# Chunk attention with a feed-forward layer: when w_in is issued, how far ahead loads go, and which blocks the crossbar transposes

## The chip, the cores and the metric

The kernel runs on one core of a Trainium2 chip. The metric is the time of one execution on the device in microseconds (us). A core has TensorE (matmuls; PE in the profile, PEld its weight loads), VectorE (DVE), ScalarE (ACT), GpSimd (POOL) and SyncE (SP, which here only issues DMAs). They run side by side, each with its own instruction list in order, and wait for each other through semaphores.

## The reference

```python
B, H, S, D = 8, 8, 576, 64; chunk = 64
scores = (1 / sqrt(D)) * q_c @ k_c.T          # within chunks of 64 tokens, per head
scores = scores - scores.max(-1, keepdims=True)
attn = exp(scores); attn = attn / (attn.sum(-1, keepdims=True) + 1e-9)
out = attn @ v_c                              # (B, H, S, D)
x = out.transpose(0, 2, 1, 3).reshape(B * S, H * D)   # 4608 x 512
h = x @ w_in                                  # w_in 512 x 2048
g = maximum(0.01 * h, h)
return g @ w_out                              # w_out 2048 x 512
```

All inputs and the output are float32.

## The kernel before

The 4608 tokens are cut into nine blocks of 512 (`NJ = 9`, `TB = 512`); a block is eight chunks of 64 over all eight heads. Heads are handled in pairs, `kk` = 0 to 3 (`NKK = 4`). A block j passes through these stages:

- `alloc(j)` takes the float32 landing tiles `qf`, `kf`, `vf` (two sets) and the float16 tiles `qh`, `kh` (two sets). `load_qk` and `load_v` (L106, L120) issue the loads, mostly from SyncE. A block seldom begins at the start of a sequence of 576, so most loads split in two: v then takes 16 issues for a block, q and k four.
- `cast_qk` and `cast_v` turn them into float16, v into `VD[j % 2]`. `VD` holds the two heads of a pair as a block diagonal, whose other half is cleared once by memsets (L65 to 67).
- `attn_t` (L174) brings q and k into the layout with the head dimension on the partitions. For j < `NPT` TensorE does this (eight transposes into the PSUM tile `tp`, from which VectorE copies `qt` and the two halves of `kd`; for block 0 ScalarE copies one half). For later blocks `transpose(j)` (L163) has issued two DMA transposes, called the crossbar here.
- `attn_s` forms the scores in `sp` and their exponential `e`; `attn_x` the sums `zp` and the product with v, `xp`, and then 1/sum on ScalarE (`lz`, `rz`); `attn_n` multiplies `xp` by `rz` on VectorE into `xT`.
- `mm1(j, fc)` is one of 16 column groups of the first product (four matmuls over `kk`), ended by ScalarE's leaky ReLU into `gT`. `mm2(j, ti, part)` is a quarter of one of four row tiles of the second product (four matmuls). After a tile's last quarter VectorE copies it into `osb` (three buffers) and SyncE stores it.

The program is written in one order by hand, and every engine runs its instructions in that order. In a block's loop n runs over 32 steps, 16 `mm1` and 16 `mm2`. Between them stand the four attention stages of the next block for each pair (`at`, from `first`, `gap` and `lags`), the loads of a later block (`loads`), the casts of block j + 2 (from step `cast_at`), and its crossbar transposes (12 steps later). Block 0's second product runs its quarters part by part over all four tiles, and so all four of its output tiles end close together; the later blocks go tile by tile.

Before the loop, block 0's attention runs pair by pair: at each step the casts of one pair, its transposes, the scores of the pair before and so on, with `keep_warm` matmuls on zeros in between and with the first three columns of the first product at the end. w_in and w_out come as float32 and land as float16 by DMAs from GpSimd, four groups each (`load_w_in(g)`, `load_w_out(g)`, 1 MB read and 512 KB written each). w_in's groups 0 to 2 are issued behind GpSimd's casts of pairs 1 to 3, and its group 3 and all of w_out after the last pair. Block 1's loads then wait for w_in's group 2 (`add_manual_dep`, L336): v first, then q and k in two halves.

Of the kernel before, what the change touches and what calls it, by code (L numbers as in the profile page):

```python
# [9 lines left out]
FP32 = mybir.dt.float32  # L10
# [5 lines left out]
def kernel(  # L16
# [9 lines left out]
    nc = tc.nc  # L26

    B, H, S, D = q.shape
# [4 lines left out]
    NKK = H // 2  # L33
# [3 lines left out]
    NC = TB // CH  # L37
    R = 4
    NI = CH // R
    NPT = 4  # L40
    SCL = float(D) ** -0.5

    sb = ctx.enter_context(tc.tile_pool(name="sb", bufs=1))
# [21 lines left out]
    for t, eng in zip(VD, (nc.vector, nc.gpsimd)):  # L65
        eng.memset(t[0:64, :, :, 1, :], 0.0)
        eng.memset(t[64:128, :, :, 0, :], 0.0)
# [88 lines left out]
    def cast_v(j, kk):  # L156
        for hh in range(2):
            rows = slice(hh * CH, (hh + 1) * CH)
            nc.gpsimd.tensor_copy(  # L159
                out=VD[j % NVD][rows, kk, :, hh, :], in_=raw[j][2][rows, kk, :, :]  # L160
            )

    def transpose(j):  # L163

# [9 lines left out]
    def attn_t(j, kk):  # L174

        if j < NPT:
            tp = psum([128, 2, R, 128], FP16, "tp", "at")
            for a in range(2):
                for r in range(R):
                    nc.tensor.transpose(  # L180
                        out=tp[:, a, r, :], in_=half[j][a][:, kk, r, :, :], identity=ident
                    )
            qt = sbuf([128, R, 128], FP16, "qt", 2)
            nc.vector.tensor_copy(out=qt, in_=tp[:, 0, :, :])  # L184
            kt = tp[:, 1, :, :]
        else:
            qt, kt = (t[:, kk, :, :] for t in trans[j])
        kd = KD[(j * NKK + kk) % NKD]
        for hh in range(2):
            p0 = hh * 64  # L190
            dst = kd[p0:p0 + 64, :, hh, :].rearrange("p c (i r) -> p c i r", r=R)
            src = kt[p0:p0 + 64, :, :].rearrange("p r (c i) -> p c i r", i=NI)
            if j == 0 and hh == 0:
                nc.scalar.activation(out=dst, in_=src, func=AFT.Copy, bias=0.0, scale=1.0)  # L194
            else:
                nc.vector.tensor_copy(out=dst, in_=src)  # L196
        live[j, kk] = (qt, kd)
# [70 lines left out]
    def mm2(j, ti, part):  # L268
        if part == 0:
            op[j, ti] = psum([128, d_model], FP32, "op", "mm")  # L270
        o = op[j, ti]
        for fc in range(part * 4, part * 4 + 4):
            nc.tensor.matmul(  # L273
                out=o,
                lhsT=gT[j][:, fc, ti * 128:(ti + 1) * 128],
                rhs=w_out[:, fc, :],
                start=(fc == 0),
                stop=(fc == NFC - 1),
            )
        if part == 3:  # L280
            osb = sbuf([128, d_model], FP32, "osb", 3)
            nc.vector.tensor_copy(out=osb, in_=o)  # L282
# [9 lines left out]
    with tc.manual_schedule():  # L292

        alloc(0)
        for kk in range(NKK):
            load_qk(0, 2 * kk, 2 * kk + 2)
        for h in range(4, H):
            load_v(0, h, nc.scalar)
        for h in range(4):
            load_v(0, h, nc.gpsimd)  # L300
        warm = psum([128, TB], FP32, "warm", "mm")
        keep_warm(10)
        w_dma = []
        hps = [psum([128, TB], FP32, "hp", "mm") for _ in range(3)]
        for step in range(NKK + 3):
            p = step - 2
            if 0 <= p < NKK:
                attn_x(0, p)
            p = step - 1
            if 0 <= p < NKK:  # L310
                attn_s(0, p)
            p = step
            if p < NKK:
                cast_qk(0, 0, p, nc.vector)
                cast_qk(1, 0, p, nc.gpsimd)
# [26 lines left out]
        for h in range(1, H):  # L342
            load_v(1, h, nc.sync)
        load_qk(1, 0, H // 2)
        load_qk(1, H // 2, H)
        for kk in range(NKK):
            cast_v(1, kk)
        for kk in range(NKK):
            cast_qk(0, 1, kk, nc.gpsimd)
            cast_qk(1, 1, kk, nc.gpsimd)  # L350

        for j in range(NJ):

            loads = {0: ((2, 16),), 1: ((3, 0), (4, 16))}.get(j, ((j + 3, 0),))

            first, gap, lags = (
                (24, 2, (0, 3, 5, 7)),
                (9, 5, (0, 3, 5, 7)),  # L360
                (6, 6, (0, 3, 5, 7)),
                (0, 7, (0, 3, 5, 7)),
            )[min(j, 3)]
            at: dict[int, list] = {}
            if j + 1 < NJ:
                for s in (3, 2, 1, 0):
                    for kk in range(NKK):
                        at.setdefault(first + gap * kk + lags[s], []).append((STEPS[s], kk))
            cast_at = (32, 24, 8, 2)[min(j, 3)]
            for n in range(NFC * 2 + (6 if j == 0 else 0)):  # L370
                if n >= 2 * NFC:
                    pass
                elif n >= NFC:
# [4 lines left out]
                for jl, n0 in loads:  # L378
                    if jl < NJ and n == n0:
                        alloc(jl)  # L380
                        load_qk(jl, 0, H)
                    if jl < NJ and n - n0 in range(1, 2 * H, 2):
# [3 lines left out]
                if j and j + 2 < NJ and n in range(cast_at, cast_at + 8, 2):  # L386
# [12 lines left out]

# [28 lines left out]
```

## Time and profile before

| | |
|---|---|
| median of three runs | 325.39 us (325.23 to 325.73) |
| profiled execution | 325.32 us, span 323.5 us, granted clock 0.968 |
| TensorE busy | 296.1 us, 92% of the span |
| VectorE, ScalarE, GpSimd busy | 111.6, 149.9, 83.8 us |
| HBM read, written | 36.70 MB, 9.44 MB |
| chain of waits by engine | PE 75%, DMA 16%, SyncE's queue 4% |

The page of the profile describes one execution. It has the busy time of each engine, the span in 40 slices of 8.09 us, and the chain of work that ended last, followed back from the last instruction. The timeline lists instructions in order of time: start, length, engine, line, operation, what is written from what, and in brackets how long the engine had been idle and for whom. A window row gives, for a stretch of time, the busy time of each engine (with the count of instructions), then the granted clock of TensorE (1.00 is full), the mean busy share of the 16 DMA engines and the GB/s they moved. Matmul ends are modelled, so lengths of single matmuls overlap; starts are what to read.

### The profile page before, as it was taken

How to read it: one execution, taken by the hardware profiler on the slowest of the kernel's cores; microseconds unless marked ns; L12 is line 12 of the kernel's file. 1: busy time of each engine (PE TensorE's matmuls, PEld its weight loads, DVE VectorE, ACT ScalarE, POOL GpSimd, SP SyncE). 2: the span in 40 equal slices, each digit the busy share in tenths (PEclk: the TensorE clock that was granted, in tenths of full speed). 3: DMA queues.
4: the chain of work that ended last, by engine and by line, in shares of the span. 5: the costliest groups of instructions: out<-in, count | busy, mean ns of one | idle time of the engine just before them, and what ended most of it. 6: DMA issues, size and time to landing. Idle time of an engine off the chain costs nothing.

```text
span 323.5 us, 4923 instructions
## 1 busy us (share of the span) xinstructions
PE 296.1 (92%) x1911; PEld 145.2 (45%) x1911; DVE 111.6 (35%) x190; ACT 149.9 (46%) x257; POOL 83.8 (26%) x136
## 2 busy tenths in 40 slices
PE   6768968729999999999999999999999999999994
PEld 2434424414555455544444454454445444444441
DVE  5450004630354155442534453424523422420011
ACT  1476400425733474258427822872385248425500
POOL 9750335461642500620810251052100000000000
PEclk9799996958999999999999999999999999999999
DMA  7999979969789599799577975995118110010011
GB/s 219 217 186 191 169 194 248 181 204 209 138 189 219 139 200 153 156 243 207 120 192 190 167 134 170 288 177 148 65 27 105 65 67 0 32 67 32 0 67 65
DMA packets 88247, 47.25 MB, mean 146 GB/s; under 512 B 61088, under 2 KB 83616, under 8 KB 88224
## 3 DMA queue, kind: packets, MB, share of 16 engines
q1 hardware_dynamic: 79776, 41.96, 58.1%
q0 software_dynamic: 6336, 4.46, 9.3%
q10 hardware_dynamic: 2112, 0.52, 0.8%
q8 instruction: 15, 0.25, 0.3%
q14 instruction: 8, 0.07, 0.1%
HBM read 36.70 MB, written 9.44 MB: 143 GB/s over the span
## 4 chain that ended last, share of the span: by engine, by line
PE 75%; DMA 16%; SPq 4%; DVE 1%; issue 1%; ACT 1%; POOL 1%; DVEq 0%; POOLq 0%; ACTq 0%
PE op L273 34%; PE hp L247 34%; DMA kf<-in_k_dram 8%; DMA vf<-in_v_dram 4%; SPq L132 2%; DMA w_in<-in_moe_w_in_dram 2%; PE zp L219 2%; PE xp L222 2%; PE sp L204 2%; DMA qf<-in_q_dram 1%; PE tp L180 1%; SPq L111 1%; DMA out_dram<-osb 1%; DVE xT L240 1%; DVE osb L282 0%
## 5 line engine op out<-in xcount | busy, mean ns | idle before, releaser
L247 PE MATMUL hp<-xT,w_in 128*128 128x512 f16 x576 | 132.9, 383 | 3.3 <-DVE xT L240 3.3
L273 PE MATMUL op<-w_out,gT 128*128 128x512 f16 x576 | 134.3, 383 | 0.0
L258 ACT ACTIVATE gT<-hp 128x512 f16<-128x512 f32 x144 | 84.9, 596 | 56.2 <-PE hp L247 56.0
L247 PEld LDWEIGHTS <-w_in 128*128 128x128 f16 x576 | 54.8, 99 | 66.1 <-issue 6.7
L273 PEld LDWEIGHTS <-gT 128*128 128x128 f16 x576 | 54.4, 99 | 59.8 <-issue 2.1
L282 DVE COPY osb<-op 128x512 f32<-128x512 f32 x36 | 24.8, 691 | 86.7 <-PE op L273 80.4
L212 ACT ACTIVATE e<-sp 128x512 f16<-128x512 f32 x36 | 21.4, 594 | 56.2 <-PE sp L204 56.0
L151 POOL CAST kh<-kf 128x512 f16<-128x512 f32 x36 | 22.5, 626 | 86.8 <-DMA kf<-in_k_dram 52.8
L240 DVE TENSOR_TENSOR xT<-xp,rz 128x512 f16<-128x512 f32 x36 | 24.7, 690 | 53.4 <-ACT rz L232 53.0
L230 ACT ACTIVATE lz<-zp 128x512 f32<-128x512 f32 x36 | 21.4, 594 | 26.7 <-PE zp L219 26.7
L184 DVE COPY qt<-tp 128x512 f16<-128x512 f16 x16 | 6.8, 423 | 62.3 <-PE tp L180 62.3
L159 POOL CAST vd_75<-vf 64x512 f16<-64x512 f32 x36 | 23.0, 638 | 19.9 <-PE xp L222 10.7
L159 POOL CAST vd_76<-vf 64x512 f16<-64x512 f32 x32 | 19.8, 618 | 25.3 <-DMA vf<-in_v_dram 19.3
L232 ACT ACTIVATE rz<-lz 128x512 f32<-128x512 f32 x36 | 22.7, 630 | 6.6 <-DVE xT L240 5.5
L219 PE MATMUL zp<-e,onesd 128*128 128x512 f16 x36 | 14.1, 392 | 7.0 <-ACT e L212 7.0
L196 DVE COPY kd_73<-kT 64x512 f16<-64x512 f16 x20 | 13.8, 690 | 0.3
L196 DVE COPY kd_74<-kT 64x512 f16<-64x512 f16 x20 | 12.5, 627 | 0.3
L180 PE MATMUL tp<-ident,kh 128*128 128x128 f16 x64 | 6.9, 237 | 3.8 <-POOL kh L151 3.8
L151 POOL CAST qh<-qf 128x512 f16<-128x512 f32 x12 | 7.3, 611 | 11.3 <-DMA qf<-in_q_dram 10.9
L196 DVE COPY kd_73<-tp 64x512 f16<-64x512 f16 x14 | 9.6, 685 | 1.5 <-ACT kd_73 L194 1.3
L196 DVE COPY kd_74<-tp 64x512 f16<-64x512 f16 x14 | 9.6, 685 | 1.5 <-ACT kd_74 L194 1.3
L222 PEld LDWEIGHTS <-vd_75 128*128 128x128 f16 x160 | 7.3, 98 | 6.2 <-issue 1.7
(40 smaller groups left out, 108.3 us busy)
## 6 DMA issues: line engine op xcount, KB each, us to landing
out_dram<-osb SPq DMA_DIRECT2D x36, 256.0 KB, 2.8
w_in<-in_moe_w_in_dram POOLq DMA_DIRECT2D x4, 512.0 KB, 8.2
w_out<-in_moe_w_out_dram POOLq DMA_DIRECT2D x4, 512.0 KB, 15.0
vf<-in_v_dram SPq DMA_DIRECT2D x16, 112.0 KB, 5.0
qf<-in_q_dram SPq DMA_DIRECT2D x6, 256.0 KB, 7.4
kf<-in_k_dram SPq DMA_DIRECT2D x6, 256.0 KB, 8.0
qf<-in_q_dram SPq DMA_DIRECT2D x2, 768.0 KB, 9.2
kf<-in_k_dram SPq DMA_DIRECT2D x2, 768.0 KB, 11.9
```

The lines of the kernel that those rows point to most:

```text
L151: eng.tensor_copy(out=half[j][a][:, kk, :, :, :], in_=raw[j][a][:, 2 * kk:2 * kk + 2, :].rearrange("p h (r d) -> p r h d", r=R),)
L159: nc.gpsimd.tensor_copy(out=VD[j % NVD][rows, kk, :, hh, :], in_=raw[j][2][rows, kk, :, :])
L196: nc.vector.tensor_copy(out=dst, in_=src)
L212: nc.scalar.activation(out=e, in_=sp, func=AFT.Exp, bias=0.0, scale=SCL)
L219: nc.tensor.matmul(out=zp, lhsT=onesd, rhs=e, start=True, stop=True)
L230: nc.scalar.activation(out=lz, in_=zp, func=AFT.Ln, bias=0.0, scale=1.0)
L232: nc.scalar.activation(out=rz, in_=lz, func=AFT.Exp, bias=0.0, scale=-1.0)
L240: nc.vector.tensor_tensor(out=xT[j][:, kk, :], in0=xp.rearrange("p r t -> p (r t)"), in1=rz, op=ALU.mult)
L247: nc.tensor.matmul(out=hp, lhsT=w_in[:, kk, fc * 128:(fc + 1) * 128], rhs=xT[j][:, kk, :], start=(kk == 0), stop=(kk == NKK - 1),)
L258: nc.scalar.activation(out=gT[j][:, fc, :], in_=hp, func=AFT.Prelu, bias=0.0, scale=1.0, alpha=0.01)
L273: nc.tensor.matmul(out=o, lhsT=gT[j][:, fc, ti * 128:(ti + 1) * 128], rhs=w_out[:, fc, :], start=(fc == 0), stop=(fc == NFC - 1),)
L282: nc.vector.tensor_copy(out=osb, in_=o)
```

## The change

In block 0, q's casts of pairs 1 to 3 move from VectorE to GpSimd, k is cast ahead of q, and v of pairs 2 and 3 is cast after the last q. w_in's group 0 is issued behind the casts of the second pair, and groups 1, 2 and 3 behind those of the third. v's heads 4 to 7 of block 0 move from ScalarE's queue to SyncE's, behind q and k; the memsets of the second `VD` move behind the issues of w_out, also on GpSimd. Block 1's q and k are loaded whole, ahead of its v, and wait for w_in's group 1 (`w_dma[1]`). ScalarE copies its half of `kd` for even pairs only. `keep_warm` runs 8 at first and then 4 at a time. `osb` has four buffers.

In the loop, block 0 loads block 2 (q and k from step 24, v from 32, behind the stores); block 1 loads block 3; block 2 loads blocks 4 and 5; and from block 3 on it is three ahead as before. The attention steps of the next block move, the last multiply to step 34 in block 0 (behind its last `mm2`), 30 in block 1, 29 in block 2, and 28 as before from block 3 on. `NPT` goes from 4 to 5, so block 4 is transposed on TensorE and only the last four blocks by crossbar, 14 steps after `cast_at`.

```diff
-    NPT = 4
+    NPT = 5
...
-            if j == 0 and hh == 0:
+            if j == 0 and hh == 0 and kk % 2 == 0:
                 nc.scalar.activation(out=dst, in_=src, func=AFT.Copy, bias=0.0, scale=1.0)
...
-            osb = sbuf([128, d_model], FP32, "osb", 3)
+            osb = sbuf([128, d_model], FP32, "osb", 4)
...
-        for h in range(4, H):
-            load_v(0, h, nc.scalar)
         for h in range(4):
             load_v(0, h, nc.gpsimd)
+        for h in range(4, H):
+            load_v(0, h, nc.sync)
...
-        keep_warm(10)
+        keep_warm(8)
...
-                cast_qk(0, 0, p, nc.vector)
                 cast_qk(1, 0, p, nc.gpsimd)
-                if p >= 2:
-                    cast_v(0, p)
-                if p >= 1:
-                    w_dma.append(load_w_in(p - 1))
+                cast_qk(0, 0, p, nc.vector if p == 0 else nc.gpsimd)
+                if p in (1, 2):
+                    w_dma += [load_w_in(g) for g in ((0,), (1, 2, 3))[p - 1]]
+                if p == 3:
+                    cast_v(0, 2)
+                    cast_v(0, 3)
                 attn_t(0, p)
...
-                keep_warm(3)
+                keep_warm(4)
...
-        w_dma.append(load_w_in(3))
-        w_dma += [load_w_out(g) for g in range(4)]
+        for g in range(4):
+            load_w_out(g)
+        clear_vd(1, nc.gpsimd)
         alloc(1)
-        first_v = load_v(1, 0, nc.sync)[0]
         tc.add_manual_dep(
-            first_v.ins,
-            w_dma[2].ins.name,
+            load_qk(1, 0, H)[0].ins,
+            w_dma[1].ins.name,
...
-        for h in range(1, H):
+        for h in range(H):
             load_v(1, h, nc.sync)
-        load_qk(1, 0, H // 2)
-        load_qk(1, H // 2, H)
-        for kk in range(NKK):
-            cast_v(1, kk)
         for kk in range(NKK):
             cast_qk(0, 1, kk, nc.gpsimd)
             cast_qk(1, 1, kk, nc.gpsimd)
+        for kk in range(NKK):
+            cast_v(1, kk)
+
+        def regular(first, gap):
+            return [[first + gap * kk + lag for kk in range(NKK)] for lag in (0, 3, 5, 7)]
...
-            loads = {0: ((2, 16),), 1: ((3, 0), (4, 16))}.get(j, ((j + 3, 0),))
-
-            first, gap, lags = (
-                (24, 2, (0, 3, 5, 7)),
-                (9, 5, (0, 3, 5, 7)),
-                (6, 6, (0, 3, 5, 7)),
-                (0, 7, (0, 3, 5, 7)),
-            )[min(j, 3)]
+            qk_at = {0: {24: 2}, 1: {0: 3}, 2: {0: 4, 16: 5}}.get(j, {0: j + 3})
+            v_at = {0: {32: 2}, 1: {1: 3}, 2: {1: 4, 17: 5}}.get(j, {1: j + 3})
+            cast_at = {0: 40, 1: 20, 2: 18}.get(j, 2)
+            steps = {
+                0: [[21, 23, 25, 27], [24, 26, 28, 30], [26, 28, 30, 32], [28, 30, 32, 34]],
+                1: regular(8, 5),
+                2: regular(1, 7),
+            }.get(j, regular(0, 7))
...
-            cast_at = (32, 24, 8, 2)[min(j, 3)]
-            for n in range(NFC * 2 + (6 if j == 0 else 0)):
+            for n in range(NFC * 2 + (16 if j == 0 else 0)):
...
-                if n == cast_at + 12 and NPT <= j + 2 < NJ:
+                if NPT <= j + 2 < NJ and n == cast_at + 14:
                     transpose(j + 2)
-            if j == 0:
-                for kk in range(NKK):
-                    cast_qk(0, 2, kk, nc.gpsimd)
-                    cast_qk(1, 2, kk, nc.gpsimd)
-                    cast_v(2, kk)
```

Three places in the order of the engines matter below. The first is GpSimd during block 0's attention, from the first casts to the weights, before:

```order
L132 DMA vd_75<-in_v_dram 64x8x64 x4
L151 CAST kh<-kf 128x512 x2
L140 DMA w_in<-in_moe_w_in_dram 128x4x512
L151 CAST kh<-kf 128x512
L159 CAST vd_75<-vf 64x8x64 x2
L140 DMA w_in<-in_moe_w_in_dram 128x4x512
L151 CAST kh<-kf 128x512
L159 CAST vd_75<-vf 64x8x64 x2
L140 DMA w_in<-in_moe_w_in_dram 128x4x512 x2
L146 DMA w_out<-in_moe_w_out_dram 128x4x512 x4
```

and now:

```order
L154 CAST kh<-kf 128x512 x2
L154 CAST qh<-qf 128x512
L143 DMA w_in<-in_moe_w_in_dram 128x4x512
L154 CAST kh<-kf 128x512
L154 CAST qh<-qf 128x512
L143 DMA w_in<-in_moe_w_in_dram 128x4x512 x3
L154 CAST kh<-kf 128x512
L154 CAST qh<-qf 128x512
L163 CAST vd_75<-vf 64x8x64 x4
L149 DMA w_out<-in_moe_w_out_dram 128x4x512 x4
L67 MEMSET vd_76 64x32x64
```

Three q casts came to GpSimd, w_in's last three groups stand two k casts earlier or more, and a memset of `VD[1]` (`vd_76`) follows w_out.

The second is SyncE from block 0's last q and k on, before (the `64x64` and `64x7x64` are block 1's v, one head in two parts):

```order
L111 DMA qf<-in_q_dram 128x2x256
L111 DMA kf<-in_k_dram 128x2x256
L132 DMA vf<-in_v_dram 64x64
L132 DMA vf<-in_v_dram 64x7x64
L132 DMA vf<-in_v_dram 64x64
```

and now (`64x8x64` is block 0's v, `16x8x256` and `112x8x256` are the two parts of block 1's q or k):

```order
L114 DMA qf<-in_q_dram 128x2x256
L114 DMA kf<-in_k_dram 128x2x256
L135 DMA vf<-in_v_dram 64x8x64 x4
L114 DMA qf<-in_q_dram 16x8x256
L114 DMA qf<-in_q_dram 112x8x256
L114 DMA kf<-in_k_dram 16x8x256
L114 DMA kf<-in_k_dram 112x8x256
L135 DMA vf<-in_v_dram 64x64
L135 DMA vf<-in_v_dram 64x7x64
```

Block 1's q and k now lead its v, and four v loads of block 0 have come to this queue.

The third is SyncE around block 0's four stores (`out_dram<-osb`), before, with the end of block 2's v around them and block 3's q behind:

```order
L132 DMA vf<-in_v_dram 64x2x64
L132 DMA vf<-in_v_dram 64x6x64
L283 DMA out_dram<-osb 128x512 x2
L132 DMA vf<-in_v_dram 64x2x64
L132 DMA vf<-in_v_dram 64x6x64
L283 DMA out_dram<-osb 128x512 x2
L132 DMA vf<-in_v_dram 64x2x64
L132 DMA vf<-in_v_dram 64x6x64
L111 DMA qf<-in_q_dram 48x8x256
```

and now, from block 2's q and k on:

```order
L114 DMA qf<-in_q_dram 32x8x256
L114 DMA qf<-in_q_dram 96x8x256
L114 DMA kf<-in_k_dram 32x8x256
L114 DMA kf<-in_k_dram 96x8x256
L285 DMA out_dram<-osb 128x512 x4
L135 DMA vf<-in_v_dram 64x2x64
L135 DMA vf<-in_v_dram 64x6x64
```

The stores stood behind twelve and fourteen of block 2's sixteen v loads, and now stand ahead of all sixteen.

More of the change, by code (lines that the diff above doesn't have):

```diff
@@ L64, with clear_vd @@
         nc.vector.memset(t[64:128, :, 0, :], 0.0)
-    for t, eng in zip(VD, (nc.vector, nc.gpsimd)):
-        eng.memset(t[0:64, :, :, 1, :], 0.0)
-        eng.memset(t[64:128, :, :, 0, :], 0.0)
+    def clear_vd(m, eng):
+        eng.memset(VD[m][0:64, :, :, 1, :], 0.0)
+        eng.memset(VD[m][64:128, :, :, 0, :], 0.0)
+    clear_vd(0, nc.vector)
     w_in = sb.tile([128, NKK, d_ff], FP16, name="w_in")
@@ L158, in cast_v @@
             rows = slice(hh * CH, (hh + 1) * CH)
-            nc.gpsimd.tensor_copy(
-                out=VD[j % NVD][rows, kk, :, hh, :], in_=raw[j][2][rows, kk, :, :]
-            )
+            dst, src = VD[j % NVD][rows, kk, :, hh, :], raw[j][2][rows, kk, :, :]
+            nc.gpsimd.tensor_copy(out=dst, in_=src)
     def transpose(j):
@@ L367 @@
                     for kk in range(NKK):
-                        at.setdefault(first + gap * kk + lags[s], []).append((STEPS[s], kk))
-            cast_at = (32, 24, 8, 2)[min(j, 3)]
-            for n in range(NFC * 2 + (6 if j == 0 else 0)):
+                        at.setdefault(steps[s][kk], []).append((STEPS[s], kk))
+            for n in range(NFC * 2 + (16 if j == 0 else 0)):
                 if n >= 2 * NFC:
@@ L377 @@
                     mm1(j, n)
[L378 to L382, printed above, removed]
+                if qk_at.get(n, NJ) < NJ:
+                    alloc(qk_at[n])
+                    load_qk(qk_at[n], 0, H)
+                for n0, jl in v_at.items():
+                    if jl < NJ and n - n0 in range(0, 2 * H, 2):
                         load_v(jl, (n - n0) // 2, nc.sync)
@@ L385 @@
                     stage(j + 1, kk)
-                if j and j + 2 < NJ and n in range(cast_at, cast_at + 8, 2):
+                if j + 2 < NJ and n in range(cast_at, cast_at + 8, 2):
                     kk = (n - cast_at) // 2
```

## The prediction

> **What bounds the kernel now.** First the page, its slices of the span:
>
> ```profile
> PE   6768968729999999999999999999999999999994
> PEclk9799996958999999999999999999999999999999
> GB/s 219 217 186 191 169 194 248 181 204 209 138 189 219 139 200 153 156 243 207 120 192 190 167 134 170 288 177 148 65 27 105 65 67 0 32 67 32 0 67 65
> ```
>
> From the tenth slice on (73 us) TensorE is full at full clock. Everything that can be won without taking matmuls away lies in the nine slices before, where digits 6 to 8 and clocks of 0.5 to 0.9 stand. The chain of what ended last, cut at the places that count:
>
> ```profile
> 1.25 4.16 DMA kf<-in_k_dram
> ...
> 16.31 6.95 DMA w_in<-in_moe_w_in_dram
> 26.64 12.12 DMA vf<-in_v_dram
> 41.42 4.82 DMA qf<-in_q_dram
> 49.02 12.66 DMA kf<-in_k_dram
> 65.02 2.75 DMA out_dram<-osb
> 73.10 9.20 PE hp L247 x37
> 82.30 0.45 PE tp L180 x8
> 105.88 0.57 issue
> 107.19 5.56 PE hp L247 x25
> 138.88 0.69 DVE osb L282
> 140.22 2.97 PE hp L247 x13
> 170.09 3.45 PE hp L247 x16
> 291.52 13.81 PE hp L247 x64
> 305.33 13.83 PE op L273 x64
> 319.18 0.69 DVE osb L282
> ```
>
> Columns: start, length, what. Up to 73.10 the chain is mostly transfers: the first k (landed at 5.4), a group of w_in, then block 1's v, its q, then block 2's k, then an output store. From 73.10 (the first product of block 1 gets its last operand) it is TensorE. I read block lengths off the starts of the first products: block 1 lasts 107.19 - 73.10 = 34.09, block 2 33.03, block 3 29.87, and blocks 4 to 7 together 291.52 - 170.09 = 121.43, so 30.36 each. One first product is 13.81 and one second product 13.83; what is left of 30.36, 2.7 us, is the next block's attention on TensorE without transposes. A block that also transposes its successor on TensorE pays four times 0.45, or 1.8.
>
> So the kernel is a start-up of 73.1 plus blocks that run close to TensorE's own work. Inside the start-up, TensorE and VectorE:
>
> ```profile
> 25.15 12.03 PE L247 MATMUL hp<-xT,w_in 128*128 128x512 f16 x55 [1.19 <-DVE xT L240]
> 47.05 0.40 PE L180 MATMUL tp<-ident,qh 128*128 128x128 f16 x4 [2.10 <-POOL qh L151]
> 49.38 0.61 PE L180 MATMUL tp<-ident,kh 128*128 128x128 f16 x4 [1.93 <-POOL kh L151]
> 67.90 0.69 DVE L282 COPY osb<-op 128x512 f32<-128x512 f32 x1 [6.02 <-DMA out_dram<-osb]
> 70.44 0.58 PE L219 MATMUL zp<-e,onesd 128*128 128x512 f16 x1 [6.24 <-ACT e L212]
> ```
>
> Block 0's products run from 25.15 without a break until the transposes of block 1 stop for q (at 47.05) and for k (at 49.38). Later comes a second stop, 6.24 us before 70.44. Its root is the fourth copy of an output tile (67.90): with three buffers it waited 6.02 us for the first store. VectorE is in order, so block 1's xT stood behind it. The store was late because of SyncE's queue:
>
> ```profile
> 23.28 17.43 SPq L132 DMA_DIRECT2D vf<-in_v_dram  x16
> 50.00 14.92 SPq L132 DMA_DIRECT2D vf<-in_v_dram  x12
> 73.92 15.69 SPq L132 DMA_DIRECT2D vf<-in_v_dram  x16
> ```
>
> Sixteen v issues hold SyncE for about 16 us, nearly 1 us each, whatever else runs. Block 1's sixteen came ahead of its q and k, and twelve of block 2's ahead of the first store at 65.02. The transfers meanwhile:
>
> ```profile
> 32.00:36.00 4.00, 4.00 (x21) 1.82 (x19) 0.00 (x0) 2.90 (x5) 0.61 (x1) 1.00 1.23 196
> 36.00:40.00 4.00, 4.00 (x20) 1.80 (x19) 0.00 (x0) 1.28 (x3) 1.67 (x3) 1.00 0.81 153
> 40.00:44.00 4.00, 4.00 (x20) 1.83 (x19) 0.00 (x0) 0.00 (x0) 2.30 (x5) 1.00 0.45 99
> 44.00:48.00 4.00, 1.35 (x9) 0.45 (x7) 0.00 (x0) 0.00 (x0) 0.91 (x2) 0.99 1.04 274
> 48.00:52.00 4.00, 2.62 (x10) 1.25 (x11) 1.71 (x3) 0.00 (x0) 2.34 (x4) 0.50 1.11 259
> ```
>
> (The last three columns are clock, DMA share, GB/s.) From 36 to 44 the DMA engines starve at 153 and 99 GB/s, because SyncE has only v to feed them, while q and k, with longer rows, later run at 274.
>
> **The change, part by part.** All times are those of the profiled execution, 325.32 us around a span of 323.5, 0.07 from the median of the runs (325.39).
>
> 1. *Attention of block 0.* The rows:
>
> ```profile
> 3.12 1.80 POOL L67 MEMSET vd_76<- 64x2048 f16 x1
> 7.79 0.61 POOL L151 CAST kh<-kf 128x512 f16<-128x512 f32 x1
> 14.53 0.61 POOL L151 CAST kh<-kf 128x512 f16<-128x512 f32 x1 [0.94 <-DMA kf<-in_k_dram]
> 18.24 0.55 DVE L151 CAST qh<-qf 128x512 f16<-128x512 f32 x1
> L151 POOL CAST qh<-qf 128x512 f16<-128x512 f32 x12 | 7.3, 611 | 11.3 <-DMA qf<-in_q_dram 10.9
> ```
>
> The first k cast starts at 7.79 without a wait of its own: GpSimd was still issuing four v loads, which stood behind two memsets of 1.80. Without these, k is cast as soon as it lands, at about 5.5 (it landed at 5.4), 2.2 us earlier. The last q cast (18.24) stood on VectorE behind an xT multiply, and now follows its k on GpSimd: three casts of 0.61 there, beside GpSimd's waits for k (0.94 ahead of 14.53). I give that 0.5. The memsets move to a place where GpSimd has nothing to do until block 1 lands; v on SyncE behind q and k frees the first transfers from half of their competition. Sum: block 0's run starts at 25.15 - 2.7 = 22.5. Bounds: nothing won (25.2), if the landing of the last k and not the chain of steps sets it; 4 us won at best, if k lands 1.3 earlier too.
>
> 2. *Weights and block 1's loads.* Three w_in groups are issued together, and block 1's q and k wait for group 1 instead of group 2. Before, group 2 landed at 16.31 + 6.95 = 23.3; one group less, 0.52 MB at 200 GB/s, is 2.6 us, so q and k are released at about 20.7. They are 2.1 MB. With the rest of the weights (3.1 MB) in flight I give them half of some 210 GB/s: 20 us, landed at 40.7. Then block 1's first q and k casts, 0.61 each, and the first transposes at about 42. TensorE would be there (six of sixteen groups, 0.86 each, into the second product) at 22.5 + 12.0 + 5.2 = 39.7, so it stops for 2.3 us. Where the weights get half, w_in's last group lands near 31 (needed at 31.5) and w_out's last near 47 (needed near 50). v comes behind q and k: some issues wait for them, the rest cost SyncE its 1 us each, so the last v lands near 51; its consumer is due at 54. Bounds: no stop, if q and k go first; or, as before, q and k land only with the last byte, at 52.8, for 13 us.
>
> 3. *The end of block 0.* The fourth output buffer takes away the 6.02, and the stores now stand ahead of block 2's v, behind only q and k. What is late next is the arithmetic tail of the last pair: from 70.44 to 73.10 it took 2.7 at half clock; I take 2.3. TensorE's work up to there is 12.0 + 13.8 + 2.7 + 1.8 = 30.3. So block 1's first product has its last operand at 22.5 + 30.3 + 2.3 (stop) + 2.3 (tail) = 57.4. Before, 73.10: **-15.7**. The same bytes had to come in by then: 2.9 MB of block 0, 4.2 of weights as written, 3.1 of block 1, together 10.2 MB, and the slices' 200 GB/s make 51 us of that, below 57.4. TensorE and the transfers are both nearly full then.
>
> 4. *Blocks 1 to 3.* Three blocks now transpose their successor on TensorE: 3 x (30.36 + 1.8) = 96.5, against 170.09 - 73.10 = 97.0 before. That the crossbar no longer does block 4 thus costs 1.8, and the two waits at block ends (105.88 to 107.19 and 138.88 to 140.22, 1.3 each) pay for it: the multiply that ended them stood at step 31 of its block and now stands at 30 and 29. For a rest of those waits and for half clock after the two pauses of 2.3 I add 1.3; bounds 0 and 5. The row from 48 to 52 shows clock 0.50 after two pauses of 2.10 and 1.93. Sum: **+0.8**.
>
> The Trainium skill, "TensorE: Matmul & The Clock Gate", section "What's actually happening", says that the gate halves the clock after an idle window of about 3.4 us. By it the pauses here would cost nothing and the sum would be about 0.8 lower; the row at 0.50, after two shorter pauses with 0.40 us of work between them, does not let me count on that.
>
> 5. *Blocks 4 to 8.* Same work, same order but for crossbar transposes two steps later: 0. They are covered by slack ahead of the next block (rival D).
>
> Sum: 325.32 - 15.7 + 0.8 = 310.4.
>
> **Rivals.**
>
> *A, forecast:* 310.4, chance 0.60.
>
> *B, block 1's q and k come late.* The DMA engines favour the weights, or the weights starve too, and TensorE stops long enough for half clock. For it: the v loads took 12.12 us beside w_out in the chain. Against: v has rows a quarter as long as q and k, so equal turns give q and k four times the rate. Landing 5 to 8 us later makes 315 to 319; I take 317. Chance 0.17.
>
> *C, the wait moves to block 2.* Its v is now issued behind four stores, and GpSimd casts q, k, v pair by pair, so a late v also stops the next pair's k. Sixteen issues from 56 at 1 us each end at 72, and the pairs are needed at about 70, 75, 80, 84 with TensorE 15.7 us earlier, so first to last they just fit. A slip of 3 to 5 us makes 314 to 316. Chance 0.09.
>
> *D, slower: crossbar transposes miss their block.* They now stand behind all sixteen v issues of a block, not fourteen, and the next block's first score needs them.
>
> ```profile
> 160.59 2.58 SPq L167 DMA_TRANSPOSE kT<-kh  x1
> ...
> kT<-kh SPq DMA_TRANSPOSE x5, 4.8
> ```
>
> Issued at 160.59 and landed 4.8 later, at 165.4, the k tile had 4.7 us until the next block at 170.09. Two v issues more take 2 of it and leave 2.7. Each us of slip beyond costs four times (blocks 5 to 8); from 3.7 us beyond, the 14.9 won are gone, which makes 325.3; with a little more, 327. Chance 0.04.
>
> *E, no effect:* block 1 still waits for the same byte, and 73.10 stands: 325.32 + 0.8, less the 1.3 that I added for pauses which then do not come, 324.8. It needs an unbroken stream; the 99 GB/s at 40 to 44 speaks against it. Chance 0.04.
>
> *F, casts on GpSimd are blocked by VectorE.* Three q casts of 0.61 each wait for a VectorE copy of about 0.7 in the chain of block 0: +2.1, 312.5. Against: twelve q casts on GpSimd average 611 ns. Chance 0.06. The rule is from the Trainium skill, "SBUF — State Buffer", section "Who interferes with whom": the two engines share a pair of ports, held for a whole instruction. The 611 does not show it.
>
> **How the numbers follow.** The likeliest is A: 310.4. The range takes in A with its bounds (4 us at best instead of 2.7 and no stop: 306.8; no win in step 1: 313.1), C and F, and most of B: 306.0 to 318.0. Left out are D, E and the upper end of B, with some of A's misses below. Faster by over 0.2% (a measurement of this kernel can tell about that from no change): A, B, C, F and some of E, 0.93; within: 0.03; slower: 0.04.
>
> **What would show it.** Step 1: the first product's long run begins near 22.5. Step 2: block 1's first transposes near 42, after at most 3 us of idle TensorE; DMA over 180 GB/s from 36 to 44. Step 3: no wait of an output copy for a store, and block 1's first product at 57 to 58. Step 4: three blocks of about 32.2. Step 5: blocks of 30.4 from block 4 on. The forecast is wrong if the first transposes of block 1 come after 46 (B), if TensorE idles for q, k or v inside block 1 (C), or if blocks from 4 on begin with a wait for a transposed tile (D).

## The result, and the profile after

The changed kernel takes 313.81 us (median of four runs, 311.98 to 314.48), the kernel before, beside it, 325.56 (325.23 to 325.84): a ratio of 0.963, 95% interval 0.9584 to 0.9677. So it is 11.7 us faster; 310.4 was forecast, with 306 to 318 around it. The profiled execution took 314.47 us, span 312.7, against 323.5 before: 10.8 us off the span, and that is what has to be accounted for. Medians and ranges here and in the table below take in every run; ratios leave out two slow runs of e3 (327.90 and 328.68).

The page after, its slices of the span:

```profile
PE   7669979799999999999969999999999999999994
PEclk9979999999999999999979999999999999999998
GB/s 195 241 206 244 247 131 184 279 110 188 175 194 223 141 168 204 144 208 196 117 247 236 109 174 205 265 201 98 36 79 91 69 34 0 36 67 34 2 67 67
```

TensorE is full from the ninth slice on (slices of 7.82 us now), not the tenth of 8.09. But there is a new mark: a 6 for TensorE and a 7 for its clock in slice 21 (156 to 164 us), a place that was full before. The chain of what ended last shows both ends of this (start, length, what):

```profile
58.95 7.28 PE hp L249 x33
...
90.60 1.73 PE hp L249 x8
...
122.74 0.86 PE hp L249 x4
...
136.44 9.78 DMA kf<-in_k_dram
...
154.77 5.30 DMA kT<-kh
...
161.42 0.61 PE sp L206 x8
...
189.77 3.45 PE hp L249 x16
...
280.84 13.81 PE hp L249 x64
```

Block 1's first product has its last operand at 58.95 instead of 73.10. Block 2 lasts 122.74 - 90.60 = 32.14. Then a transfer stands in the chain where before only TensorE stood: kT, block 5's transposed keys, landed at 160.07. Blocks 3 and 4 together last 189.77 - 122.74 = 67.03; with 32.14 for a block that transposes its successor on TensorE and 30.36 for one that doesn't they would last 62.50. So 4.5 us are lost there. Behind 189.77 nothing differs: 91.07 to the last block, as before.

Block 5 began later in the kernel before, by its chain:

```profile
200.45 3.45 PE hp L247 x16
```

The sum: 73.10 to 58.95 is -14.15; block 1's first product to block 5's lasts 189.77 - 58.95 = 130.82 instead of 200.45 - 73.10 = 127.35, which is +3.5, made of the +4.5 of block 4 and -1.1 in blocks 1 to 3; the end brings -0.1. Together -10.8, the whole of it.

The start-up and block 4 on TensorE, from the timeline (start, length, line, operation, idle time before it and whom it waited for):

```profile
17.25 1.45 PE L249 MATMUL hp<-xT,w_in 128*128 128x512 f16 x3 [1.85 <-DMA w_in<-in_moe_w_in_dram]
...
23.55 12.03 PE L249 MATMUL hp<-xT,w_in 128*128 128x512 f16 x55 [1.19 <-DVE xT L242]
...
42.73 0.40 PE L182 MATMUL tp<-ident,kh 128*128 128x128 f16 x4 [1.75 <-POOL kh L154]
...
154.72 3.62 PE L249 MATMUL hp<-xT,w_in 128*128 128x512 f16 x16
161.42 0.61 PE L206 MATMUL sp<-qT,kd_73 128*128 128x64 f16 x8 [3.08 <-DVE kd_73 L198]
```

The same kernel's VectorE and SyncE, from the timeline of each:

```profile
56.03 0.69 DVE L284 COPY osb<-op 128x512 f32<-128x512 f32 x1 [0.26 <-PE op L275]
...
160.16 1.21 DVE L198 COPY kd_73<-kT 64x512 f16<-64x512 f16 x2 [4.54 <-DMA kT<-kh]
```

```profile
20.08 0.83 SPq L114 DMA_DIRECT2D qf<-in_q_dram  x2
20.95 1.03 SPq L114 DMA_DIRECT2D kf<-in_k_dram  x2
22.03 26.70 SPq L135 DMA_DIRECT2D vf<-in_v_dram  x16
...
53.09 3.99 SPq L285 DMA_DIRECT2D out_dram<-osb  x4
...
137.07 16.05 SPq L135 DMA_DIRECT2D vf<-in_v_dram  x16
153.23 1.44 SPq L169 DMA_TRANSPOSE qT<-qh  x1
154.77 3.47 SPq L169 DMA_TRANSPOSE kT<-kh  x1
```

The fourth output copy (56.03) waits 0.26 us, for TensorE, where it waited 6.02 for a store. At 160.16 VectorE waits for kT: the transposes stand behind the sixteen v loads of block 6 and went out at 153.23 and 154.77, when block 4 had already begun. The windows (busy time of PE, PEld, DVE, ACT, POOL, then clock, DMA share, GB/s):

```profile
36.00:40.00 4.00, 4.00 (x21) 1.82 (x19) 0.00 (x0) 0.21 (x1) 0.00 (x0) 1.00 1.16 257
40.00:44.00 4.00, 2.25 (x17) 1.18 (x16) 0.83 (x2) 0.00 (x0) 1.94 (x4) 1.00 0.77 155
...
160.00:164.00 4.00, 2.58 (x14) 1.18 (x15) 2.27 (x5) 0.82 (x2) 0.00 (x0) 0.58 1.09 253
```

DMA is no longer starved from 36 to 40 (257 GB/s, 153 before). Behind the 3.08 us stop for kT TensorE runs at a clock of 0.58; stop and half clock together are the 4.5.

### The profile page after: what moved, and what is told of

Same layout as the page of the kernel before. It is cut to its first block, busy times and chain, and to the rows that moved or that the text cites. A ratio compares the mean times of both kernels' runs of the same rounds, so it can differ in the third digit from the quotient of the medians.

```text
span 312.7 us, 4993 instructions
## 1 busy us (share of the span) xinstructions
PE 293.9 (94%) x1944; PEld 145.8 (47%) x1944; DVE 114.2 (37%) x193; ACT 148.6 (48%) x255; POOL 85.5 (27%) x139
## 4 chain that ended last, share of the span: by engine, by line
PE 74%; DMA 12%; SPq 9%; DVE 1%; ACT 1%; issue 1%; POOL 1%; DVEq 0%
PE op L275 33%; PE hp L249 32%; SPq L135 8%; DMA kf<-in_k_dram 5%; DMA w_in<-in_moe_w_in_dram 3%; PE sp L206 2%; PE zp L221 2%; PE tp L182 2%; PE xp L224 2%; SPq L114 2%; DMA vf<-in_v_dram 2%; DMA kT<-kh 2%; ACT lz L232 1%; DVE kd_74 L198 0%; ACT rz L234 0%
## 5 line engine op out<-in xcount | busy, mean ns | idle before, releaser
L275 PE MATMUL op<-w_out,gT 128*128 128x512 f16 x576 | 132.3, 379 | 0.0
L186 DVE COPY qt<-tp 128x512 f16<-128x512 f16 x20 | 8.5, 425 | 43.9 <-PE tp L182 43.7
L154 POOL CAST qh<-qf 128x512 f16<-128x512 f32 x15 | 9.2, 615 | 17.4 <-DMA qf<-in_q_dram 17.0
L198 DVE COPY kd_74<-tp 64x512 f16<-64x512 f16 x20 | 13.7, 684 | 0.3
L198 DVE COPY kd_73<-tp 64x512 f16<-64x512 f16 x18 | 12.3, 685 | 1.6 <-ACT kd_73 L196 1.3
L198 DVE COPY kd_73<-kT 64x512 f16<-64x512 f16 x16 | 10.2, 639 | 4.8 <-DMA kT<-kh 4.5
L206 PEld LDWEIGHTS <-kd_73 128*128 128x128 f16 x144 | 6.6, 99 | 9.4 <-DVE kd_73 L198 5.6
L198 DVE COPY kd_74<-kT 64x512 f16<-64x512 f16 x16 | 10.3, 642 | 0.3
L224 PEld LDWEIGHTS <-vd_75 128*128 128x128 f16 x160 | 7.6, 100 | 5.0 <-issue 0.6
## 6 DMA issues: line engine op xcount, KB each, us to landing
qf<-in_q_dram SPq DMA_DIRECT2D x2, 896.0 KB, 10.8
kf<-in_k_dram SPq DMA_DIRECT2D x2, 896.0 KB, 16.2
```

Source lines behind the costliest of these rows:

```text
L154: eng.tensor_copy(out=half[j][a][:, kk, :, :, :], in_=raw[j][a][:, 2 * kk:2 * kk + 2, :].rearrange("p h (r d) -> p r h d", r=R),)
L275: nc.tensor.matmul(out=o, lhsT=gT[j][:, fc, ti * 128:(ti + 1) * 128], rhs=w_out[:, fc, :], start=(fc == 0), stop=(fc == NFC - 1),)
```

## The experiments

Each kernel is either kernel with one thing altered, or a kernel of this list with one thing altered. Block 1 and block 5 stand for the start of their first products in the profiled execution (us).

| kernel | median (range), us | ratio to before, 95% | block 1 | block 5 |
|---|---|---|---|---|
| before (its page) | 325.39 | | 73.10 | 200.45 |
| after | 313.81 (311.98-314.48) | 0.963 (0.9584-0.9677) | 58.95 | 189.77 |
| e1_before_osb4 | 325.74 (324.56-327.72) | 1.0013 (0.9993-1.0033) | 63.92 | 200.39 |
| e2_after_osb3 | 321.00 (319.81-324.08) | 0.9881 (0.984-0.9923) | 63.14 | 196.15 |
| e3_after_v_first | 325.55 (321.93-328.68) | 0.9984 (0.9952-1.0016) | 70.27 | 200.97 |
| e4_after_crossbar_first | 310.31 (309.95-312.06) | 0.9546 (0.9512-0.9579) | 58.92 | 185.22 |
| e5_before_osb4_npt5 | 319.58 (318.75-320.84) | 0.9834 (0.9784-0.9884) | 65.67 | 194.13 |
| e6_after_npt6 | 312.41 (311.99-314.32) | 0.9622 (0.9571-0.9673) | 59.49 | 187.58 |
| e7_crossbar_first_npt4 | 309.23 (307.32-310.59) | 0.9508 (0.9449-0.9567) | 61.51 | 186.02 |
| e8_crossbar_first_old_prelude | 310.67 (310.29-311.62) | 0.9553 (0.9503-0.9603) | 60.61 | 186.91 |
| e9_crossbar_first_stores_behind_v | 310.26 (309.61-311.61) | 0.9534 (0.9512-0.9557) | 59.26 | 185.56 |
| e10_crossbar_first_again | 310.72 (309.48-312.09) | 0.9541 (0.9512-0.9571) | 60.86 | 187.16 |
| e11_old_prelude_again | 310.27 (309.86-311.05) | 0.9535 (0.9514-0.9556) | 58.88 | 185.17 |
| e12_npt4_again | 309.07 (308.02-310.32) | 0.9490 (0.9466-0.9513) | 58.93 | 183.44 |

e1 to e4 shared one chip and its runs of before, e5 to e8 another set, e9 to e12 a third.

### The late crossbar: e4, e6

e4 issues a block's transposes as soon as its casts are through, ahead of the next loads instead of behind them:

```diff
-            qk_at = {...}.get(j, {0: j + 3})
-            v_at = {...}.get(j, {1: j + 3})
+            qk_at = {...}.get(j, {10: j + 3})
+            v_at = {...}.get(j, {11: j + 3})
...
-                if NPT <= j + 2 < NJ and n == cast_at + 14:
+                if NPT <= j + 2 < NJ and n == cast_at + 7:
```

> The changed kernel with the crossbar transposes of a block, from block 5 on, issued right behind its casts (step 9 of its loop) and the next loads behind them (q and k from step 10, v from 11). Theory (block 4 lost 4.7 us because block 5's two transposes stood behind sixteen v issues): block 4 is back to 30.4 from 35.1, 309 to 310.5 and less spread between runs. Rival (the casts of block 5 are late themselves, its loads came too late): block 4 still waits for kT, 313 to 315. Second rival (the loads that are now later make a new wait): a stop for k or v in blocks 5 to 7, 311 to 314.

310.31 us, 3.5 below the changed kernel, and no wait for kT is left: VectorE copies kT at the time at which it gets there by itself.

```profile
155.51 1.71 DVE L198 COPY kd<-kT 64x512 f16<-64x512 f16 x2
```

So the 4.5 us of block 4 were the place of the transposes in SyncE's queue, and e4 wins them back (185.22 against 189.77 at block 5). That row also dates the need: 155.5. Before, the same copy stood at 170.74, and kT landed at 165.4:

```profile
170.74 1.22 DVE L196 COPY kd_73<-kT 64x512 f16<-64x512 f16 x2
```

In the changed kernel kT landed at 160.07.

e6 takes the crossbar away from block 5 in another manner, `NPT = 6`.

> Changed kernel with block 5 transposed on TensorE as well. Theory: the 4.7 us that block 4 lost to block 5's crossbar transposes go, 1.8 us of transposing come (32.1 against 30.36 us a block): 313.8 - 4.7 + 1.8 = 310.9, range 310.2-312, block 4 lasts 32.1 us. Rival (the late crossbar moves on to block 6, whose transposes also stand behind 16 loads of v): no gain, 313 or more, with a wait for kT in block 5.

312.41, with block 4 at 187.58 - 155.43 = 32.15 and no wait for kT anywhere. Mechanism right, gain smaller than expected: at block 5 it is 2.2 us ahead of the changed kernel in place of 2.7, since this execution was already 0.5 behind at block 1; the medians differ by 1.4, inside the scatter of either. The rival is out: block 6's transposes come in time.

### The fourth buffer, alone and taken away: e1, e2

e1 is the kernel before with `osb` at 4 buffers instead of 3, nothing else.

> The kernel before with four osb buffers instead of three, nothing else. Theory (the second stop in block 0 was a buffer wait): the 6.02 us of the fourth output copy go, block 1's xT is no longer held, block 1's first product gets its last operand near 66.5 instead of 73.1, 318.5 to 320 us. Rival (the start-up ends when the last bytes of block 1 and 2 are in, whatever waits in between): at most 1 us is won, 324.4 or more.

The total did not move (ratio 1.0013), as the rival had it, but not for the rival's reason. Timeline of e1, TensorE and SyncE's queue:

```profile
63.92 8.45 PE L247 MATMUL hp<-xT,w_in 128*128 128x512 f16 x31 [0.36 <-DVE xT L240]
...
140.39 0.61 PE L204 MATMUL sp<-qT,kd 128*128 128x64 f16 x8 [5.83 <-DVE kd L196]
```

```profile
113.28 17.70 SPq L132 DMA_DIRECT2D vf<-in_v_dram  x16
...
131.67 2.93 SPq L167 DMA_TRANSPOSE qT<-qh  x1
134.70 1.92 SPq L167 DMA_TRANSPOSE kT<-kh  x1
```

Block 1 came 9.2 us earlier (63.92), and 8.6 of it was still there at block 3 (131.59 against 140.22). Then block 3 stopped 5.83 us for block 4's kT, whose transposes SyncE issued at 131.67 and 134.70; before, it had issued them at 132.86 and 135.17, of which the second:

```profile
135.17 2.60 SPq L167 DMA_TRANSPOSE kT<-kh  x1
```

TensorE had moved by 9 us and SyncE's queue by one half to one. By block 5 e1 stands where before stood, to within 0.1.

e2 is the changed kernel with `osb` back at 3.

> The changed kernel with three osb buffers again. Theory (the stores now stand ahead of block 2's v, which alone frees a buffer in time): the first store issues near 53.1 and lands near 56, when the fourth copy came (56.03), so 0 to 1 us is lost, 313.5 to 315. Rival (the fourth buffer is what the change won): the old wait of 6 us is back, 319 or more.

The rival was right: +7.2 us by the medians. VectorE of e2:

```profile
61.20 0.69 DVE L284 COPY osb<-op 128x512 f32<-128x512 f32 x1 [3.46 <-DMA out_dram<-osb]
...
132.18 0.69 DVE L284 COPY osb<-op 128x512 f32<-128x512 f32 x1 [5.22 <-DMA out_dram<-osb]
```

and the transfers that its chain names there:

```profile
55.06 6.02 DMA out_dram<-osb
...
122.53 9.54 DMA out_dram<-osb
```

I had taken 2.8 us for a store, the median; with block 2's q and k ahead of it, it took 6.02, and 9.54 in block 2. (The median hides such stores in other kernels too: the longest took 9.3 us before, and 9.5 in the changed kernel, where no copy waited for it.) So the fourth buffer is needed even though the stores stand ahead of v. Not all of the +4.2 at block 1 is the buffer's: e2's stop for k was 2.94 us, with a clock of 0.56 from 43 to 46 behind it, which costs 1.7 us (below), and its first k transpose came 0.3 later (43.01 against 42.73), so the buffer's share there is about 2.2.

### Before with the fourth buffer and one more block on TensorE: e5

e1 with `NPT = 5`.

> Kernel before with a fourth output buffer (as in e1_before_osb4) and block 4 transposed on TensorE as well. Theory: e1_before_osb4 brought block 1's first product from 73.10 to 63.92 us and lost it again to block 4's crossbar transposes, which landed 7.6 us late; with block 4 on TensorE that wait is gone, block 4's transposes also leave SyncE's queue (some 4.5 us), and the 9.2 us stay except 1.8 us of added transposing: 325.3 - 9.2 + 1.8 = 317.9, range 316.5-319.5, block 4's first matmul near 163. Rival (SyncE's queue of loads is full and sets the pace): the wait moves to block 5's transposes (near 160 us in the queue, needed near 163), and the time is 321 or more.

319.58: 6.2 below e1, no wait for kT left, and block 4 to block 5 lasts 194.13 - 163.77 = 30.36. The rival is out. The theory's 317.9 was missed by 1.7, and block 1 comes 1.75 later in the profiled execution than in e1 (65.67 against 63.92). There the transposes of block 1 stopped for 1.24 and 1.55 us, and the clock of the window from 48 to 52 was 0.67; in e1, with one stop of 2.80, the same window stood at 1.00.

### The order of block 1's loads: e3

```diff
         tc.add_manual_dep(
-            load_qk(1, 0, H)[0].ins,
+            load_v(1, 0, nc.sync)[0].ins,
...
-        for h in range(H):
+        for h in range(1, H):
             load_v(1, h, nc.sync)
+        load_qk(1, 0, H)
```

> The changed kernel with block 1's v issued ahead of its q and k again, released by the same w_in group. Theory (the order of block 1's loads is a main part of the gain, since sixteen slow v issues hold q and k back): q and k land near 48 instead of 42, block 1's first product comes 4 to 6 us later at partly half clock, 318 to 320. Rival (all bytes of block 1 are needed in any case, so their order is worth nothing): 313 to 315.

+11.7 us by the medians, well above the theory. TensorE of e3:

```profile
47.68 0.61 PE L182 MATMUL tp<-ident,qh 128*128 128x128 f16 x4 [7.68 <-POOL qh L154]
51.94 0.61 PE L182 MATMUL tp<-ident,kh 128*128 128x128 f16 x4 [3.65 <-POOL kh L154]
```

TensorE stops for 7.68 and again for 3.65 us, and the window from 44 to 56 has a clock of 0.50. So the order is worth about 11 us in this kernel (70.27 against 58.95 at block 1).

e1 has v first as well, and yet its block 1 comes at 63.92. The first k transpose is at 48.31 there and at 51.94 in e3, though both issue their first k of block 1 at nearly the same time (40.08 and 40.19). What differs is that e1, like the kernel before, loads q and k in two halves, so its first k is half as large; e3 loads them whole. That this is the reason for the 3.6 us is likely, but no run changes it alone. The other 2.7 us lie between that transpose and block 1's first product (15.6 us in e1, 18.3 in e3), behind stops that left the clock at 1.00 in e1 and at 0.50 in e3. From e1 to the changed kernel everything in which they differ is together worth 63.92 - 58.95 = 5.0 at block 1.

### The prelude: e8, e10, e11

e8 is e4 with block 0's prelude as before: q casts on VectorE, w_in one group behind each of pairs 1 to 3, v's upper heads on ScalarE's queue, the second memset early, `keep_warm` and ScalarE's `kd` copies as they were, block 1's loads behind the third w_in group. Block 1's q and k stay ahead of its v.

> e4_after_crossbar_first with the prelude of the kernel before (q casts on VectorE, w_in group by group behind pairs 1 to 3, v's upper heads on the ScalarE queue, block 1's loads behind the third w_in group). Theory: the long run of first products begins 1.6 us later (25.15 against 23.55) and block 1's q and k are issued 3.2 us later (23.28 against 20.08), so block 1's transposes are late too: 310.3 + 1.6 to + 5, that is 312-315.5. Rival (the prelude is covered by what follows, block 1's loads end at the same time): 311 or less.

The profile agreed with the theory (block 1 at 60.61, 1.7 later) and the median did not (0.4). Both kernels were run again, side by side:

> The same kernel as e4_after_crossbar_first (310.31 us), on this chip in more rounds, to stand beside the other three: 309.5-311.5 us, ratio 0.951-0.958.

> The same kernel as e8_crossbar_first_old_prelude, in more rounds. There the profile showed block 1's first product 1.7 us later than with the new prelude (60.61 against 58.92) and the medians only 0.4 us. Theory (the 1.7 us reach the end): 1.2-2.2 us above e10_crossbar_first_again. Rival (they are regained later): within 0.7 us of it.

310.72 with the new prelude, 310.27 with the old one: the theory is out, and no gain from the prelude can be seen here. TensorE of e10 (new prelude), then of e11 (old one):

```profile
22.44 12.03 PE L249 MATMUL hp<-xT,w_in 128*128 128x512 f16 x55 [1.19 <-DVE xT L242]
...
42.97 0.40 PE L182 MATMUL tp<-ident,kh 128*128 128x128 f16 x4 [3.09 <-POOL kh L154]
...
60.86 1.46 PE L249 MATMUL hp<-xT,w_in 128*128 128x512 f16 x6 [1.19 <-DVE xT L242]
```

```profile
25.26 12.03 PE L250 MATMUL hp<-xT,w_in 128*128 128x512 f16 x55 [1.19 <-DVE xT L243]
...
42.66 0.40 PE L183 MATMUL tp<-ident,kh 128*128 128x128 f16 x4
...
58.88 3.40 PE L250 MATMUL hp<-xT,w_in 128*128 128x512 f16 x15 [1.19 <-DVE xT L243]
```

In e10 the long run began 2.8 us earlier and block 1 came 2.0 us later. Block 1's first k is cast at about 42 in both (42.30 and 41.99; in e8 it was 43.73), so a quicker block 0 only makes TensorE wait for it: 3.09 us in e10, none in e11. And half clock followed e10's wait. The window from 43 to 46, e10:

```profile
43.00:46.00 3.00, 3.00 (x12) 1.25 (x13) 1.71 (x3) 0.00 (x0) 3.00 (x6) 0.58 0.43 95
```

### The place of the stores: e9

e4 with block 2's loads queued from step 16 of block 0 on (q and k at 16, v from 17), as before, with the four buffers kept:

```diff
-            qk_at = {0: {24: 2}, ...}
-            v_at = {0: {32: 2}, ...}
+            qk_at = {0: {16: 2}, ...}
+            v_at = {0: {17: 2}, ...}
```

> e4_after_crossbar_first with block 2's loads queued from step 16 of block 0 on, as before, so that block 0's stores stand among and behind them; four output buffers stay. Theory: with four buffers no copy of block 0 waits for a store, so where the stores stand costs nothing: block 1's first product at 58.9 +- 0.7 us, the time within 0.8 us of e10_crossbar_first_again beside it. Rival (the place of the stores was worth something by itself): a wait for a store to land in block 0 or 1, first product 60.5 or later, or 2 us or more in all.

310.26 against 310.72 for e10, block 1 at 59.26: no effect, though the stores went out at 65.18 and 67.63, where in the changed kernel the first went at 53.09. With four buffers it doesn't matter whether the stores stand ahead of v.

### Block 4 by crossbar, in time: e7, e12

```diff
-    NPT = 5
+    NPT = 4
...
-            cast_at = {0: 40, 1: 20, 2: 18}.get(j, 2)
+            cast_at = {0: 40, 1: 20, 2: 9}.get(j, 2)
...
-                if NPT <= j + 2 < NJ and n == cast_at + 7:
+                if NPT <= j + 2 < NJ and n == cast_at + (6 if j == 2 else 7):
```

(Taken from e4; block 5's loads follow the transposes.)

> e4_after_crossbar_first with block 4 transposed by crossbar as well, its casts at steps 9 to 15 of block 2 and its transposes at step 15, ahead of block 5's loads. Theory: a block whose successor comes by crossbar lasts 30.36 us, not 32.1, and the transposes land near 117 us, before block 3 begins near 122.7: 310.3 - 1.8 = 308.5, range 307.8-309.5. Rival (SyncE's queue is full up to there): kT of block 4 lands after 122.7, with a wait for kT in block 3, and the time is 310.3 or more.

309.23 falls short of the 308.5; the profiled execution had a start-up like e10's (block 1 at 61.51). Run again beside e10:

> The same kernel as e7_crossbar_first_npt4, in more rounds. Theory (block 4 by crossbar in time is worth the transposing of one block): 1.8 us below e10_crossbar_first_again, 1.0-2.4. Rival: within 0.7 us of it.

309.07 against 310.72: -1.65, as expected. In the profiles block 5 comes 1.78 us earlier than in e4 (183.44 against 185.22), with block 1 at the same time. SyncE's queue of e12:

```profile
112.12 2.84 SPq L169 DMA_TRANSPOSE qT<-qh  x1
115.07 2.41 SPq L169 DMA_TRANSPOSE kT<-kh  x1
```

Block 4's kT goes out at 115.07, ahead of block 5's loads, and block 3 begins at 122.73 and lasts 30.36 (the next begins at 153.09). This is the fastest kernel of the study, ratio 0.949 (0.9466 to 0.9513). By e11 and e9 the old prelude and the old place of the stores should do as well in it; that combination was not run.

## Why the prediction was right, and where it was not

**Step 1, block 0's attention: -2.7, its size wrong and its place in the sum too.** The long run began at 23.55, not 22.5: the first k cast did come early, at 4.51, but TensorE then waited 1.85 us for w_in's first group (row 17.25). That cost nothing, because the -2.7 could not reach the end. The prediction added the start of the run and a stop for k as if each were given; yet the stop was defined by k's arrival, and an earlier run makes the stop longer by as much. By its own numbers a run that began at 25.2 would have had no stop, and block 1 would have come at 57.8 in place of 57.4. The bound "no win in step 1: 313.1" was wrong by that; e10 and e11 showed it. Rival F, GpSimd's casts held up by VectorE, did not come: the three q casts that moved took 0.62, 0.61 and 0.64 us, and the group row has fifteen q casts on GpSimd at 615 ns, against 611 for twelve before. The Trainium skill, "SBUF — State Buffer", section "Who interferes with whom", has a lock of the shared ports for a whole instruction; no q cast on GpSimd here shows one. Some later k casts do run longer beside VectorE's copies of kT: the one at 180.90 took 0.86 us instead of 0.61, while two copies from 180.43 took 1.80 instead of 1.22.

**Step 2, the order of block 1's loads: right; its earlier release shows no gain.** q and k were issued at 20.08 (forecast 20.7), the first k transpose came at 42.73 (42), with a stop of 1.75 us (2.3) and 257 GB/s from 36 to 40; 155 from 40 to 44 is below the 180 asked for: block 1's k was in by 42.06, and what SyncE still issued was v, up to 48.7. e3 shows that the order carries the result. The release behind an earlier w_in group shows no gain: with the later one the first k is cast at 41.99 (e11) and 43.73 (e8), with the earlier one at 42.30 (e10), and the medians agree within 0.5. Counted in k casts, w_in's group 1 stands where it stood and groups 2 and 3 one cast earlier, not "two k casts earlier or more". And "nearly 1 us each, whatever else runs" does not hold for the v issues: in the row at 22.03 sixteen took 26.70 us, with a median of 0.63 and a longest of 4.97.

**Step 3, the end of block 0: right, 1.5 us too short.** No output copy waits for a store; block 1 at 58.95 against 57.4. From the first k transpose to block 1 it took 16.2 instead of the 15.4 in the sum, and the transpose came 0.7 late. Of the two causes that the step named only one counts: the buffer (e2). The stores ahead of v bring nothing beside it (e9).

**Step 4, blocks 1 to 3: mechanism right, its 1.3 for waits not needed.** 130.82 - 4.5 - 30.36 = 95.9 for three blocks where 97.8 was forecast: block 1 lasts 90.60 - 58.95 = 31.65, blocks 2 and 3 32.14 each, without a stop. Half clock behind a pause had no place in this term, since it stands ahead of block 1's first product where it occurs (e10); here the single stop for k of 1.75 us left the clock at 1.00. The two waits at block ends are gone. They are still there in e5, which has the old steps and `NPT = 5` (blocks 1 and 2 last 33.4 and 33.0); moving the steps was not tried alone.

**Step 5, blocks 4 to 8: the step that failed.** "0. They are covered by slack ahead of the next block" was +4.5. Rival D named the mechanism, transposes behind sixteen v loads, but sized its slack from the kernel before, 4.7 us less two loads, as though the transposes would move ahead with TensorE. They did not: kT was needed 15.2 us earlier (170.74 to 155.51) and landed 5.3 earlier (165.4 to 160.07). SyncE's queue of loads goes at its own pace; in the changed kernel it has hardly a gap from 100 to 181 us. And it missed once, not four times: when block 6's kT was issued, at 183.37, block 5 began at 189.77. D's price of a fall below before was therefore far off too, while its chance, 0.04, was too low for a slip of some us. By the prediction's own last sign, blocks from 4 on that begin with a wait for a transposed tile, this step was wrong, and the range had left D out. That the time lies in the range all the same is partly luck: the slip came once and cost 4.5 us.

The errors add up, with one against the others: +1.5 in steps 1 to 3, -1.9 in step 4, +4.5 in step 5 make 4.1, and the profiled execution came 314.47 - 310.4 = 4.1 above the forecast.

The rule weighed in step 4 can be set against more stops now. The time from the first k transpose of block 1 to block 1's first product is 16.2 us in e4, e12, e8, e9, the changed kernel and e6, after stops of 0.75, 1.35, 1.52, 1.53, 1.75 and 2.07 us, and 17.9 in e7 and e10, after 2.34 and 3.09. The rows of e6, then of e7:

```profile
43.28 0.40 PE L182 MATMUL tp<-ident,kh 128*128 128x128 f16 x4 [2.07 <-POOL kh L154]
```

```profile
43.62 0.40 PE L182 MATMUL tp<-ident,kh 128*128 128x128 f16 x4 [2.34 <-POOL kh L154]
```

and their windows behind it, one of e6 and then two of e7:

```profile
43.00:46.00 3.00, 2.72 (x22) 1.67 (x23) 1.82 (x4) 0.00 (x0) 3.00 (x7) 1.00 0.44 97
```

```profile
43.00:46.00 3.00, 2.38 (x11) 1.08 (x12) 1.71 (x3) 0.00 (x0) 3.00 (x6) 0.78 0.39 88
46.00:48.00 2.00, 2.00 (x12) 1.31 (x11) 0.45 (x2) 0.00 (x0) 1.94 (x4) 0.50 0.34 75
```

The stop of 2.07 us left the clock at 1.00; the one of 2.34 was followed by 0.50 and cost 1.7 us more. It is no plain threshold, for in e1 a stop of 2.80 left it at 1.00:

```profile
48.31 0.40 PE L180 MATMUL tp<-ident,kh 128*128 128x128 f16 x4 [2.80 <-POOL kh L151]
```

```profile
48.00:52.00 4.00, 3.69 (x33) 2.19 (x34) 2.76 (x6) 0.00 (x0) 2.17 (x5) 1.00 1.13 243
```

What decides between 2.1 and 3.1 us stays open. The Trainium skill, "TensorE: Matmul & The Clock Gate", section "What's actually happening", has the clock halved after an idle window of about 3.4 us, and calls that window free-running, so that its effect varies from run to run. The variation agrees with e1, e6 and e7; the 3.4 us as a length that must be idle do not, since single stops of 2.34 and 3.09 us had half clock behind them. No run here shows the windows themselves. That the 1.7 us also make most of the scatter between runs of one kernel (308.02 to 310.32 in e12) is likely, but was not shown, as only one run of each was profiled.

## What to carry to other kernels

When a change makes the compute engine earlier, the queues that feed it later do not get earlier by themselves: for each later transfer set the new time of need against the old time of issue, and put what is needed first ahead of bulk loads (e4). A term that moves the start of a stretch that ends in a wait for something else is worth nothing; take the later of the two, do not add them (e11). And a small change alone can show nothing because its gain is eaten further on: e1's 9 us appeared only once block 4's crossbar was out of the way (e5).

## What the runs showed of the hardware that was not expected

- A store of 256 KB took 6.02 and 9.54 us behind loads of the same queue, where the median is 2.8 (e2).
- Sixteen v issues fill some 16 us of SyncE's queue, but they are not 1 us of work each: in the changed kernel seven of block 6's sixteen fill the time from 137.07 until its k has landed (136.44 + 9.78 = 146.2), and the nine behind it, in the chain, go at 0.6 us each but for one of 1.63.
- Single stops of TensorE of 2.34, 2.94 and 3.09 us had half clock behind them, worth 1.7 us, and one of 2.80 (e1) did not; the same kernel's block 1 came at 58.92 or 60.86 (e4, e10).
